# Moving batch loads, an activation and checks in a one-core attention and MLP kernel

One change to a tuned Trainium2 kernel: the last load of batch 1 is issued from the ScalarE queue and the load before it one place earlier, all loads of batch 3 are issued in one go where they had been handed out one by one between the matmuls, two tanh activations of batch 2 are set behind the relu that they stood in front of, and a numerical check is spread over three units of work.

## The chip, the cores and the metric

The kernel runs on one core of one Trainium2 chip. The metric is the device time of one execution in microseconds (us). Most executions of a kernel agree closely (before: 101.72 to 102.07 us). Some are called slow: they come out longer, many of them with a lower granted TensorE clock (kernel 10 below: one run of 103.56 us at a clock of 0.975, beside three of 99.58 to 99.62 us at 0.996 to 1.000). The profile is taken in one further execution; its span, from the first to the last instruction, is about 2 us shorter than the time of the same execution (100.2 against 102.19 us in before).

Engine names: PE is TensorE, DVE is VectorE, ACT is ScalarE, POOL is GpSimd, SP is SyncE. "SPq" and "ACTq" are the DMA issues of SP and of ACT. L357 is line 357 of the kernel.

## The reference, cut to what matters

```python
# B=4 batches, H=8 heads, S=768 positions, D=40: an mLSTM-like attention
for t in range(S):
    m_new = maximum(f[t] + m, i[t])
    C = exp(f[t] + m - m_new) * C + exp(i[t] - m_new) * outer(v[t], k[t])
    n = exp(f[t] + m - m_new) * n + exp(i[t] - m_new) * k[t]
    m = m_new
    y[t] = sigmoid(o_gate[t]) * (C @ q[t]) / maximum(abs(n @ q[t]), 1)
# y becomes x, 3072 tokens of 320 values; then a maxout MLP, d_ff = 1024
out = maximum(x @ w1, x @ w2) @ w_out
```

## The kernel before

The kernel works through chunks of 128 positions, n = 0 to 23, six of them to a batch. `ph` is the matmul that reads the state with q (`C @ q`); `pu` and `po` are the two layers of the MLP, which fill TensorE for most of the time. Before `ph(n)` can run, q has to be loaded, cast to bf16 by GpSimd, and transposed. From n = 8 on, most pairs of chunks are transposed by a DMA on the SP queue (`x_q` below), some on TensorE (`f_q`).

The loads of one batch are six DMAs. A "first" load moves 1024 runs of 160 bytes (160 KB). A "rest" load moves 1024 runs of 800 bytes (800 KB). I call them *narrow* and *wide* below.

```python
def load_first(b, src, store, name, eng):                       # narrow
    t = stage(b, store, name)
    eng.dma_start(out=t[:, :, 0, :], in_=src[b, :, 0:L, :].rearrange("h p d -> p h d"))

def load_rest(b, src, store, name, eng):                        # wide
    t = stage(b, store, name)
    eng.dma_start(out=t[:, :, 1:NT, :].rearrange("p h c d -> p h (c d)"),
                  in_=src[b, :, L:S, :].rearrange("h (p c) d -> p h (c d)", c=REST))

def load_batch(b, eng):          # k, v, q first, gate first, q rest, gate rest
    return [lambda: load_kv(b, b + 1, k, kst, eng), lambda: load_kv(b, b + 1, v, vst, eng),
            lambda: load_first(b, q, qst, "qst", eng), lambda: load_first(b, o_gate, ost, "ost", eng),
            lambda: load_rest(b, q, qst, "qst", eng), lambda: load_rest(b, o_gate, ost, "ost", eng)]
# ... cut ...
def x_q(n):                      # transposes q of the pair n, n+1 by DMA
    b, c = bc(n)
    # ... cut ...
    SP.dma_start(out=qT[b][:, c:c + 2].rearrange("p c s t -> p (c s) t"),
                 in_=qp[b % 2][:, c:c + 2].rearrange("p c s d -> p (c s d)"), transpose=True)
```

The order of everything is written out by a loop over units of work. A list `late` holds pieces that are issued one at a time, one at each call of `fronts` (several calls to a unit). `A` is ScalarE, `V` VectorE, `G` GpSimd.

```python
def cross(n):
    x_q(n)
    done[("q", n)] = clock[0] + 6        # from here ph(n) may be scheduled
late = []
def fronts(limit, cap=1):
    clock[0] += 1
    if late:
        late.pop(0)()
    # ... cut: issues what is ready of q, h, y, k, c ...
# ... cut ...
sigm(1, 0, 1)                    # tanh of the gate on ScalarE
sig_first(1, V)                  # gate scaling on VectorE
for n in (8, 10):
    cross(n)
late += load_batch(2, A)
# ... cut ...
for u in range(FIRST, NU + 1):
    if u == 2:
        # ... cut ...
        late += [lambda: None] * 8 + [lambda: cross(14), lambda: cross(16)]
        sigm(2, 0, 1)
        sig_first(2, V)
        sigm(2, 1, 3)
        sigm(2, 3, 6)
    # ... cut ...
    for half in range(2):
        # ... cut ...
            for _ in up(u, half, then=rows_):        # pu and its relu
                fronts(max(u + 1, 3), 2 if u < 2 else 1)
            if u == 2 and half == 0:
                late += load_batch(3, A)
        if u == NU - 1:
            (check_gates, check_den)[half](*[1][half:])
        if u == NU and half == 0:
            check_flag()
        for _ in down(u - 1, s0, s1):                # po
            fronts(max(u + 1, 3), 2 if u < 2 else 1)
    if u == NU - 2:
        check_gates(0)
```

The checks test on the chip whether the inputs allow the fast formulas; with these inputs they do.

## Time and profile before

| | before |
|---|---|
| median of 3 runs | 101.96 us (101.72 to 102.07) |
| span of the profiled run | 100.2 us |
| TensorE busy | 89.2 us |
| granted TensorE clock | 1.000 |

From the page of the kernel before: busy time of each engine, then TensorE's busy share in 40 equal slices, in tenths, and the granted clock in the same slices.

```profile
PE 89.2 (89%) x846; PEld 63.3 (63%) x846; DVE 54.3 (54%) x160; ACT 42.5 (42%) x63; POOL 28.6 (29%) x67
...
PE   4999978988997959989999998999999999989930
...
PEclk9999999999999999999999999999999999999999
```

TensorE is busy in nine tenths of nearly every slice, at full clock. So the time of this kernel is TensorE's work plus TensorE's waits, and a wait of another engine costs nothing unless it ends in one of TensorE.

These are matmuls from TensorE's timeline of before. The columns are start, duration, engine, line, operation, output and inputs, shapes and count; in brackets, how long TensorE had been idle, and what ended that.

```profile
31.53 0.33 PE L341 MATMUL ps<-qT,kT 120*126 120x128 bf16 x3 [0.53 <-DVE qT L299]
...
34.87 0.32 PE L357 MATMUL ph<-cq,qT 120*128 120x123 bf16 x3 [0.17 <-DMA qT<-qb]
...
37.44 0.32 PE L357 MATMUL ph<-cq,qT 120*128 120x123 bf16 x3 [1.12 <-DMA qT<-qb]
...
44.82 0.60 PE L460 MATMUL pu<-xT,wd 128*128 128x256 bf16 x4 [0.36 <-ACT gt L477]
...
49.44 0.32 PE L357 MATMUL ph<-cq,qT 120*128 120x123 bf16 x3
...
50.78 0.31 PE L357 MATMUL ph<-cq,qT 120*128 120x123 bf16 x3
...
60.82 0.60 PE L460 MATMUL pu<-xT,wd 128*128 128x256 bf16 x4 [0.38 <-DMA xT<-y]
...
89.45 0.69 PE L485 MATMUL po<-Wc_t,xT 64*128 64x320 bf16 x2 [0.28 <-DVE o_sb L499]
```

The six with brackets are the waits that the change is after: for a VectorE copy of qT (31.53), for DMA transposes of q (34.87 and 37.44), for a relu on ScalarE (44.82), for the DMA transpose of y (60.82), and for the copy `o_sb` (89.45). The two at 49.44 and 50.78 are read-outs of pairs 14 and 16: no bracket, so their transposes were in time. The view of waits gives the sum of all waits for q's transposes, as total us, number, and the longest:

```profile
PE ph L357 <- DMA qT<-qb: 1.3, 2, 1.1
```

Next, DMA issues from the timeline of all engines. The second column is how long the issuing engine was occupied; x2 means two issues in a row.

```profile
45.35 2.54 SPq L287 DMA_TRANSPOSE qT<-qb  x2
...
47.83 0.40 ACTq L94 DMA_DIRECT2D qst<-in_q_dram  x1
...
48.94 0.79 ACTq L98 DMA_DIRECT2D qst<-in_q_dram  x1
...
49.77 0.63 ACTq L98 DMA_DIRECT2D ost<-in_o_gate_dram  x1
...
51.06 3.20 SPq L380 DMA_TRANSPOSE xT<-y  x2
```

Pairs 14 and 16 are transposed at 45.35, in a gap: two loads of batch 3, k and v, were issued before (42.3 and 42.7), the narrow ones follow at 47.83, and the wide ones at 48.94 and 49.77. The last line is two transposes of y, issued behind the wide loads. The second of them was issued at 53.02 and landed at about 60.7, so 7.7 us after its issue, against a median of 2.6.

Last, VectorE near the end: the check's reduction waits for GpSimd's subtraction, and the copy `o_sb`, which TensorE waits for, stands behind it.

```profile
87.54 0.90 DVE L527 TENSOR_REDUCE viol<-a 32x1 f32<-32x726 f32 x1 [1.64 <-POOL a L522]
...
88.90 0.89 DVE L499 COPY o_sb<-po 128x320 f32<-128x320 f32 x2
```

### The profile page before, as it was taken

The numbers are of one execution on the slowest core, as the hardware profiler recorded it, in microseconds if no ns is written. First come the engines' busy times: TensorE is split into PE (matmuls) and PEld (weight loads), VectorE is DVE, ScalarE is ACT, GpSimd is POOL, SyncE is SP. The second block draws the span as 40 slices with busy tenths as digits, with TensorE's granted clock in tenths as the row PEclk, the third lists the DMA queues.
The fourth block names the chain that finished last, engine by engine and source line by source line (L and its number), as shares of the span: only waits on it lengthen the run. The fifth ranks groups of instructions, "written<-read, shape, count | busy, mean of one in ns | idle before, by whom it ended". The sixth has DMA issues, their size and how long they took to land.

```text
span 100.2 us, 2241 instructions
## 1 busy us (share of the span) xinstructions
PE 89.2 (89%) x846; PEld 63.3 (63%) x846; DVE 54.3 (54%) x160; ACT 42.5 (42%) x63; POOL 28.6 (29%) x67
## 2 busy tenths in 40 slices
PE   4999978988997959989999998999999999989930
PEld 1356566755686737767867776777676767757610
DVE  5979648543648748865373117772161116395510
ACT  0897685545246450192715086431607071340000
POOL 6044797565255330914020800000000000610000
PEclk9999999999999999999999999999999999999999
DMA  0999999998995999926999999749633201103331
GB/s 17 191 293 355 384 386 365 313 170 139 322 351 136 194 284 347 319 41 155 158 210 368 177 185 313 155 126 65 146 131 65 106 32 70 61 0 134 131 115 35
DMA packets 37311, 18.91 MB, mean 189 GB/s; under 512 B 25648, under 2 KB 35952, under 8 KB 37296
## 3 DMA queue, kind: packets, MB, share of 16 engines
q1 hardware_dynamic: 26138, 14.34, 55.0%
q10 hardware_dynamic: 11158, 4.38, 18.8%
q8 instruction: 8, 0.13, 0.6%
q14 instruction: 7, 0.06, 0.2%
HBM read 12.42 MB, written 3.93 MB: 163 GB/s over the span
## 4 chain that ended last, share of the span: by engine, by line
PE 37%; DMA 32%; SPq 10%; issue 5%; POOL 5%; DVE 5%; ACT 1%; ACTq 1%; POOLq 0%
PE po L496 14%; PE pu L460 11%; DMA xT<-y 8%; DMA ost<-in_o_gate_dram 7%; DMA kst<-in_k_dram 7%; DMA w<-in_moe_w_dram 6%; SPq L104 5%; DMA qT<-qb 5%; PE po L492 4%; PE pu L468 3%; SPq L118 3%; PE ph L357 2%; POOL a L522 2%; DVE o_sb L499 2%; DVE F L520 1%
## 5 line engine op out<-in xcount | busy, mean ns | idle before, releaser
L460 PE MATMUL pu<-xT,wd 128*128 128x256 bf16 (+1 forms) x224 | 25.9, 257 | 1.8 <-ACT gt L477 0.7
L477 ACT ACTIVATE gt<-pu 128x1024 bf16<-128x1024 f32 x18 | 17.5, 1020 | 23.1 <-PE pu L468 23.1
L496 PE MATMUL po<-wo,gt 128*128 128x320 bf16 x160 | 26.6, 299 | 0.0
L499 DVE COPY o_sb<-po 128x320 f32<-128x320 f32 x22 | 10.7, 489 | 22.7 <-PE po L496 21.0
L460 PEld LDWEIGHTS <-wd 128*128 128x128 bf16 x224 | 18.8, 98 | 5.1 <-issue 1.7
L496 PEld LDWEIGHTS <-gt 128*128 128x128 bf16 x160 | 15.1, 98 | 5.4
L265 ACT ACTIVATE ost<-ost 128x320 f32<-128x320 f32 (+2 forms) x14 | 8.7, 656 | 8.5 <-DMA ost<-in_o_gate_dram 8.4
L367 DVE SCALAR_TENSOR_TENSOR y<-ost,ph 128x320 bf16<-128x320 f32 x20 | 9.7, 483 | 4.7 <-PE ph L357 4.7
L492 PE MATMUL po<-Wc_t,xT 128*128 128x320 bf16 x48 | 10.5, 301 | 0.0
L255 POOL CAST qb<-qst 128x240 bf16<-128x240 f32 (+1 forms) x12 | 6.1, 506 | 15.4 <-DMA qst<-in_q_dram 15.4
L220 PE MATMUL pd<-warm,ident_b 128*128 128x512 bf16 x25 | 8.6, 469 | 1.4 <-POOL ident_b masks.py:199 1.4
L522 POOL TENSOR_TENSOR a<-i_sb,F 32x640 f32<-32x640 f32 x1 | 1.5, 1527 | 28.2 <-DVE F L520 28.2
L468 PE MATMUL pu<-xT,wd 64*128 64x256 bf16 (+1 forms) x112 | 7.7, 256 | 0.0
L477 ACT ACTIVATE gs<-pu 128x512 bf16<-128x512 f32 x8 | 4.3, 591 | 7.7 <-PE pu L468 5.3
L357 PE MATMUL ph<-cq,qT 120*128 120x123 bf16 (+1 forms) x60 | 6.0, 214 | 1.6 <-DMA qT<-qb 1.3
L357 PEld LDWEIGHTS <-qT 120*128 120x128 bf16 (+1 forms) x60 | 4.1, 98 | 4.1 <-DMA qT<-qb 1.8
L398 POOL TENSOR_TENSOR wd<-w 128x512 bf16<-128x512 f32 x4 | 5.1, 1269 | 2.5 <-DMA w<-in_moe_w_dram 2.4
L468 PEld LDWEIGHTS <-wd 64*128 64x128 bf16 x112 | 4.0, 94 | 2.6 <-issue 1.7
L492 PEld LDWEIGHTS <-xT 128*128 128x128 bf16 x48 | 3.7, 97 | 2.9 <-issue 1.9
L496 PE MATMUL po<-wo,gs 128*128 128x320 bf16 x32 | 5.2, 299 | 0.0
L220 PEld LDWEIGHTS <-ident_b 128*128 128x128 bf16 x25 | 2.5, 115 | 3.5 <-issue 1.7
L485 PE MATMUL po<-Wc_t,xT 64*128 64x320 bf16 x24 | 3.9, 297 | 0.8 <-ACT Wc_t L438 0.4
(126 smaller groups left out, 108.8 us busy)
## 6 DMA issues: line engine op xcount, KB each, us to landing
out_dram<-o_sb SPq DMA_DIRECT2D x24, 160.0 KB, 3.1
w<-in_moe_w_dram SPq DMA_DIRECT2D x8, 256.0 KB, 5.5
qst<-in_q_dram ACTq DMA_DIRECT2D x2, 800.0 KB, 6.5
ost<-in_o_gate_dram ACTq DMA_DIRECT2D x2, 800.0 KB, 10.5
wo_st<-in_moe_w_out_dram SPq DMA_DIRECT2D x2, 640.0 KB
qst<-in_q_dram SPq DMA_DIRECT2D x1, 800.0 KB
ost<-in_o_gate_dram SPq DMA_DIRECT2D x1, 800.0 KB
wx<-in_moe_w_dram SPq DMA_DIRECT2D x2, 256.0 KB
```

What stands on the lines that cost most here:

```text
L220: nc.tensor.matmul(pd[:, 0, :], ident_b, warm, start=True, stop=True)
L255: cp(eng)(out=qp[b % 2][:, c0:c1, 0:2, 0:HS3 * D].rearrange("p c s (h d) -> p c s h d", d=D), in_=qst[b][:, 0:6, c0:c1, :].rearrange("p (s ...
L265: A.activation(out=s, in_=s, func=AF.Tanh, scale=0.5)
L357: nc.tensor.matmul(ph[:, vcols(s), :].rearrange("p a b -> p (a b)"), lhsT, rhs[:, vcols(s), :].rearrange("p a b -> p (a b)"), start=True, ...
L367: V.scalar_tensor_tensor(out=yo, in0=ost[b][:, :, c, :], scalar=1.0, in1=ph[:, :, 0:D], op0=OP.add, op1=OP.mult)
L398: eng.tensor_tensor(out=wd[:, c, half * 512:half * 512 + 512], in0=t[:, 0, c], in1=t[:, 1, c], op=OP.subtract)
L460: nc.tensor.matmul(pus[i][:, j, :], wd[:, c, f * 128:(f + 1) * 128], x[:, :, GA[i][c], :], start=(c == 0 and (j % 2 == 0 if np_ == 2 else ...
L468: nc.tensor.matmul(pus[i][:, j, :], wd2[r, f * 128:(f + 1) * 128], x[r, :, 2, :], start=False, stop=(j == 3 if np_ == 1 else j % 2 == 1))
L477: A.activation(out=o, in_=pus[i], func=AF.Relu)
L492: nc.tensor.matmul(po, x[:, s // 2, GA[s % 2][cc], :], Wc_t[:, cc, :], start=False, stop=False)
L496: nc.tensor.matmul(po, gt[:, f, s % 2, s // 2 * L:(s // 2 + 1) * L], wo[:, f, :], start=False, stop=(f == NFF - 1))
L499: cp(eng)(out=o_sb, in_=po)
```

## The change

The intent is to take away these waits: gate rest of batch 1 leaves the SP queue so that q of batch 1 arrives earlier; the tanh no longer holds the relu; batch 3's loads are done before y's transposes come; the checks no longer hold the copies. The diff, cut to its core:

```diff
-    for piece in load_batch(1, SP):
-        piece()
+    for j in (0, 1, 2, 4, 3):
+        load_batch(1, SP)[j]()
...
     f_q(4, A)
+    load_batch(1, A)[5]()
...
     def emit(op):
+        if op[:2] == ("q", NT):
+            sig_first(1, V)
...
     sigm(1, 0, 1)
-    sig_first(1, V)
     for n in (8, 10):
         cross(n)
...
             sigm(2, 0, 1)
             sig_first(2, V)
-            sigm(2, 1, 3)
-            sigm(2, 3, 6)
...
                 if u == 2 and half == 0:
-                    late += load_batch(3, A)
+                    sigm(2, 1, 3)
+                    sigm(2, 3, 6)
+                    for piece in load_batch(3, A):
+                        piece()
-            if u == NU - 1:
-                (check_gates, check_den)[half](*[1][half:])
-            if u == NU and half == 0:
-                check_flag()
+            if u == NU - 1 and half == 0:
+                late += [lambda: None] * CP + [check_abs] + [lambda: None] * 2 + [check_low] + [lambda: None] * 5 + [check_flag]
...
-        if u == NU - 2:
-            check_gates(0)
+        if u == NU - 2:
+            late += [lambda: None] * CV + [check_viol]
+        if u == NU - 3:
+            check_gates()
```

Cut: the check's functions are divided into `check_gates`, `check_viol`, `check_abs` and `check_low`, with the same instructions; `CP = 1`, `CV = 12`; in the code, `check_viol` stands ahead of the loop over halves.

More of the change, by code (lines that the diff above doesn't have):

```diff
@@ L514, with check_gates, check_viol @@
     flag_i = const.tile([1, 1], I32, name="flag_i")
-    def check_gates(part):
-        if part == 0:
-            V.memset(ones_b, 1.0)
-            V.memset(ok_b, 0.0)
-            V.tensor_tensor_scan(out=F[:, L:S], data0=ones[:, L:S], data1=f_sb[:, L:S], initial=F[:, L - 1:L],
-                                 op0=OP.mult, op1=OP.add)
-            G.tensor_tensor(out=a[:, L:S], in0=i_sb[:, L:S], in1=F[:, L:S], op=OP.subtract)
-            G.memset(bnd, 0.5)
-            G.tensor_scalar(out=bnd.rearrange("p (b c) h -> p b c h", c=NT)[:, :, 0, :],
-                            in0=gT[:, 1, :].rearrange("p (b h) -> p b h", b=B), scalar1=0.5, scalar2=None, op0=OP.mult)
-            return
+    def check_gates():
+        V.memset(ones_b, 1.0)
+        V.memset(ok_b, 0.0)
+        V.tensor_tensor_scan(out=F[:, L:S], data0=ones[:, L:S], data1=f_sb[:, L:S], initial=F[:, L - 1:L],
+                             op0=OP.mult, op1=OP.add)
+        G.tensor_tensor(out=a[:, L:S], in0=i_sb[:, L:S], in1=F[:, L:S], op=OP.subtract)
+        G.memset(bnd, 0.5)
+        G.tensor_scalar(out=bnd.rearrange("p (b c) h -> p b c h", c=NT)[:, :, 0, :],
+                        in0=gT[:, 1, :].rearrange("p (b h) -> p b h", b=B), scalar1=0.5, scalar2=None, op0=OP.mult)
+    def check_viol():
         V.tensor_reduce(out=viol[:, 0:1], in_=a[:, T0:S], axis=AX.X, op=OP.max)
@@ L532, in check_gates, with check_abs, check_low @@
         V.tensor_tensor(out=ok_b[0:BH, 0:1], in0=viol[:, 1:2], in1=viol[:, 2:3], op=OP.mult)
-    def check_den():
-        ab = ewp.tile([128, B * NT, H], FP, name="ab", tag="ab", bufs=1)
+    ab = const.tile([128, B * NT, H], FP, name="ab")
+    def check_abs():
         V.scalar_tensor_tensor(out=ab, in0=nqb, scalar=-1.0, in1=nqb, op0=OP.mult, op1=OP.max)
+    def check_low():
         V.tensor_tensor(out=ab, in0=bnd, in1=ab, op=OP.subtract)
@@ L698 @@
     XL = 3
+    CP = 1
+    CV = 12
     WX = 12
```

## The prediction

The sum is -1.1 - 0.36 + 0.6 - 0.38 - 0.28 = -1.52 us, and 101.96 less that is the 100.5.

> **What bounds the kernel now.** TensorE: 89.2 us busy of a 100.2 us span (busy table), clock full. After 25 us its matmuls run back to back, and their order is the same in both kernels except for one tiny flag matmul. So only TensorE's waits can be won. Its timeline shows: 0.53 us at 31.5 (scores wait for a VectorE copy of qT), 0.17 at 34.9 and 1.12 at 37.4 (read-out `ph` waits for qT's DMA transposes), 0.36 at 44.8 (`pu` waits for a relu on ScalarE), 0.38 at 60.8 (`pu` waits for the DMA transpose of y), 0.28 at 89.5 (`po` waits for o_sb), and two of 0.25 that the change does not touch. About 2.8 us are within reach.
>
> **The change, step by step.**
> 1. Batch 1. In the SP queue q rest now precedes gate first; gate rest goes to the ACT queue at about 24.6 us. In the trace the 160-byte first pieces take about 1.1 us of DMA each, so q rest should land near 27.4 instead of 28.6, and GpSimd's casts end near 29.8 instead of 31.05. The gate scaling (VectorE, 0.58 us) moves behind the qT copy, which removes the 0.53 us. The second qT transpose (issued 32.5, landed 37.4) can be issued near 31.3, before batch 2's loads fill the DMA. The first is held by an output store ahead of it and gains 0.2. Estimate: 1.1 us (0.3 to 1.8). Gate rest lands as before (30.9).
> 2. tanh of batch 2 behind the relu: ScalarE waited 4.5 us in it for the gate load until 42.2. The 0.36 us goes, and does not grow although TensorE arrives earlier.
> 3. Batch 3 loaded in one go near 42 to 46 instead of 42 to 50.4. Gain: the y transposes at 51 to 54 no longer share with it (the second landed 7.7 us after y; the median is 2.6), so the 0.38 us goes. Cost: the qT transposes of pairs 14 and 16 (issued 45.4 and 46.7, in a gap of the loads) now share with 160-byte packets. [...]beside batch 2's loads a qT transpose landed 4.5 to 4.9 us after issue, against a median of 2.8. I expect new `ph` waits there, 0.3 to 1.2 us, estimate 0.6.
> 4. Checks spread: scan (1.5), GpSimd subtract (1.5) and reduce (0.9) held the o_sb copy until 88.9; now the 0.28 us goes. The scan delays the last y by 1.5 us, with some 8 us of slack. Nothing is added; the tail is unchanged.
>
> Sum: -1.1 - 0.36 + 0.6 - 0.38 - 0.28 = about -1.5. 101.96 becomes **100.5 us**, 8 in 10 between 99.6 and 101.5. Faster by over 2%: 0.23; within 2%: 0.75; slower: 0.02.
>
> **What would show each step.** (1) the wait at 37.4 falls below 0.6, the first large batch-1 cast starts before 28.0, no `ps` wait. (2) no `pu` wait for a relu near 43. (3) batch 3's gate rest lands before 55 instead of 60.3; no `pu` wait for the y transpose; new `ph` waits near 48 to 50, or none. (4) no `po` wait for o_sb at the end.
>
> **What would make it wrong.** [...]the casts come no earlier: step 1 is worth nothing, total 101.5. Or batch 3's burst holds the qT transposes longer than 1.2 us. On the other side, if batch 1's qT transposes run ahead of batch 2's loads and those of pairs 14 and 16 lose nothing, all 2.8 us are won: 99.2.

## The result

Ratios in this document are the mean time of one kernel's fast runs over that of the kernel before in the same rounds, so they are not quite the ratios of the medians quoted. Below 1 is faster than before.

| | before | after |
|---|---|---|
| median of 4 runs | 101.84 us (101.3 to 102.07) | 107.19 us (106.74 to 107.36) |
| span of the profiled run | 100.2 us | 105.3 us |
| TensorE busy | 89.2 us | 91.1 us |
| granted clock, mean | 1.000 | 0.965 |

The ratio is 1.0527 (95% interval 1.047 to 1.0583). The kernel became slower by 5.3%, and the prediction of 100.5 us was wrong. The clock of 0.965 is not the slow state: all four runs of after have 0.960 to 0.965.

The page of after, the same three lines:

```profile
PE 91.1 (87%) x846; PEld 63.9 (61%) x846; DVE 55.2 (52%) x160; ACT 42.5 (40%) x63; POOL 28.4 (27%) x67
...
PE   4999798997999579996329999999999999999940
...
PEclk9999999999999999999965599999999999999999
```

TensorE's row has a hole in the slices from about 50 us on, and the clock's row has one at about the same place. The clock records of the trace say that the granted clock was 0.5 from 53.58 to 60.40 us, which is 6.83 us.

TensorE's timeline of after, at the places shown for before:

```profile
34.58 0.32 PE L357 MATMUL ph<-cq,qT 120*128 120x123 bf16 x3 [0.53 <-DMA qT<-qb]
...
37.27 0.32 PE L357 MATMUL ph<-cq,qT 120*128 120x123 bf16 x3 [1.24 <-DMA qT<-qb]
...
51.84 0.33 PE L357 MATMUL ph<-cq,qT 120*128 120x123 bf16 x3 [2.63 <-DMA qT<-qb]
...
52.44 0.32 PE L357 MATMUL ph<-cq,qT 120*128 120x123 bf16 x3
...
55.23 0.46 PE L357 MATMUL ph<-cq,qT 120*128 120x123 bf16 x3 [2.04 <-DMA qT<-qb]
```

The waits at 31.5, 44.8, 60.8 and 89.5 of before are gone. The two for batch 1's transposes (34.58 and 37.27) have stayed. The two read-outs that had waited for nothing now wait 2.63 and 2.04 us. In the view of waits:

```profile
PE ph L357 <- DMA qT<-qb: 6.4, 4, 2.6
```

The DMA issues at this place in after:

```profile
43.92 0.40 ACTq L94 DMA_DIRECT2D qst<-in_q_dram  x1
...
45.00 0.75 ACTq L98 DMA_DIRECT2D qst<-in_q_dram  x1
...
45.18 2.95 SPq L287 DMA_TRANSPOSE qT<-qb  x2
...
45.79 1.14 ACTq L98 DMA_DIRECT2D ost<-in_o_gate_dram  x1
```

All of batch 3's loads are now issued from 42.1 to 46.9 us, and q rest, the first wide one, is handed over at the same time as the first transpose (45.18), gate rest at the time of the second (46.54).

Two stretches of time: stretch, its length, busy time (and instructions) of PE, PEld, DVE, ACT and POOL, granted clock, DMA share and GB/s. First before, then after.

```profile
49.00:56.00 7.00, 7.00 (x69) 5.26 (x67) 3.99 (x13) 2.61 (x3) 0.94 (x3) 1.00 1.06 265
56.00:62.00 6.00, 5.62 (x53) 4.01 (x51) 1.76 (x4) 3.93 (x5) 1.81 (x6) 1.00 1.24 224
```

```profile
49.00:56.00 7.00, 2.33 (x22) 1.65 (x21) 2.21 (x7) 0.28 (x1) 2.17 (x6) 0.83 1.14 290
56.00:62.00 6.00, 6.00 (x38) 3.44 (x37) 1.53 (x6) 1.94 (x2) 0.00 (x0) 0.63 0.22 30
```

From 49 to 56 us TensorE did 2.33 us of work where it had done 7.00. From 56 to 62 it was fully busy, with 38 matmuls where before there were 53: that is the lower clock (0.63 on average in this stretch), not a wait.

When the same matmul of both traces is compared all along, after minus before is -0.40 us at 46.3 us, +2.40 at the read-out of 49.4, +4.45 at that of 50.8, +6.83 at before's 53.5, +6.31 at 60.8, +6.10 at 72.8, +5.65 at 89.45 and +5.26 at the end. So all of the loss arises within 8 us of before's timeline, in two terms: 4.67 us of waits for the transposes of pairs 14 and 16, and 2.4 us of work at half clock. The rest of the change won about 2 us.

Why were the transposes late? I counted the DMA packets that began in each stretch of 0.5 us: the transposes of q are 768 packets of 256 bytes each, a wide load is 1024 packets of 800 bytes. Before, both transposes ran alone; in after they did not:

```
packets begun    before: 256 B  800 B      after: 256 B  800 B
46.5 to 47.0         364      0                    0      0
47.0 to 47.5         386      0                  183      1
47.5 to 48.0          67      0                  263     19
48.0 to 48.5         419      0                  183     83
48.5 to 49.0         298      0                   74     92
49.0 to 49.5           2      0                   65    136
49.5 to 50.0           0      0                    0    191
50.0 to 50.5           0      0                    0    196
50.5 to 51.0           0     31                   16    190
51.0 to 51.5           0     40                   52    173
51.5 to 52.0           0    141                   57    114
52.0 to 52.5           0    168                   42     51
52.5 to 53.0           0    183                  149    148
53.0 to 53.5           0    178                  162    165
53.5 to 54.0           0    194                  170    163
```

In after the first transpose moves beside the end of the narrow loads and the start of q rest, the second hardly gets a packet while q rest moves, and then shares one to one with gate rest. The two were late in different ways. The first one's data packets began 1.9 us after its issue (1.2 in before) and had all begun by 49.48; but the 32 packets of 4 bytes that follow a transpose's data (in before, 32 behind each of the two) began only between 49.35 and 51.19 (47.38 to 47.64 in before), and it landed at 51.80. The second one's data began 4.0 us after its issue, when 737 of q rest's 1024 packets had begun. So they landed 6.6 and 8.6 us after their issue, where before's took 2.8 and 2.9.

### The profile page after: what moved, and what is told of

Same layout as the page of the kernel before. It is cut to its first block, busy times and chain, and to the rows that moved or that the text cites. A ratio compares the mean times of both kernels' runs of the same rounds, so it can differ in the third digit from the quotient of the medians.

```text
span 105.3 us, 2243 instructions
## 1 busy us (share of the span) xinstructions
PE 91.1 (87%) x846; PEld 63.9 (61%) x846; DVE 55.2 (52%) x160; ACT 42.5 (40%) x63; POOL 28.4 (27%) x67
## 4 chain that ended last, share of the span: by engine, by line
PE 47%; DMA 39%; SPq 6%; ACTq 1%; DVE 1%; issue 1%; ACT 1%; DVEq 0%
PE po L496 20%; DMA ost<-in_o_gate_dram 16%; DMA qT<-qb 13%; PE pu L460 12%; PE po L492 6%; DMA w<-in_moe_w_dram 6%; PE pu L468 5%; DMA qst<-in_q_dram 2%; SPq L118 2%; PE ph L357 2%; DMA kst<-in_k_dram 2%; SPq L104 2%; PE po L485 1%; ACTq L82 1%; SPq L111 1%
## 5 line engine op out<-in xcount | busy, mean ns | idle before, releaser
L496 PE MATMUL po<-wo,gt 128*128 128x320 bf16 x160 | 27.6, 306 | 0.0
```

The costliest lines, as they stand in the source:

```text
L496: nc.tensor.matmul(po, gt[:, f, s % 2, s // 2 * L:(s // 2 + 1) * L], wo[:, f, :], start=False, stop=(f == NFF - 1))
```

## The experiments

At this point I had three questions. Is the burst the whole loss, or do other parts share in it? Is the half clock a consequence of the waits, or a cause of its own? And what makes a transpose late: does a wide load in flight take turns with it (so that it is slowed), or does it go ahead of it (so that it has to wait), or is the end of a transpose tied to the loads in some other way? The quoted texts number the theories as they stood then; a theory or rival in them is a guess that the run was to test.

The kernels ran in four calls, each on one chip, with 7 runs of the kernel before beside them (medians 102.39, 101.8, 102.36 and 103.1 us). As before's median differs from call to call by over 1%, ratios of different calls should not be compared more closely than that.

### 1. After, with batch 3 loaded piece by piece as before

```diff
-                    for piece in load_batch(3, A):
-                        piece()
+                    late += load_batch(3, A)
```

> The changed kernel with one part undone: batch 3's six loads are again handed out one by one between the matmuls, instead of in one go. Theory 1 (the burst of loads holds up the qT transposes of pairs 14 and 16, and the clock drop follows from the waits): both waits at those ph (2.63 and 2.04 us) go to zero, the clock stays at 1.0, and the time is 101.0 to 101.4, slightly better than before, since the relu and o_sb waits (0.36, 0.28) stay away. Rival (moving the gate load of batch 1 to the ACT queue, or the checks, costs the time): stays above 105.

Measured: 100.70 us (100.41 to 101.14), ratio 0.9823 (0.9765 to 0.9881). The clock of the profiled run is 1.000, and the waits at pairs 14 and 16 are gone. What stays is 0.59 and 1.42 us for batch 1's transposes, 0.40 for a y, and 0.17 for the y transpose. So the burst alone turns a kernel that is 1.8% faster than before into one that is 5.3% slower.

### 2. Before, with the burst only

```diff
-                    late += load_batch(3, A)
+                    for piece in load_batch(3, A):
+                        piece()
```

> The kernel before with one part added: batch 3's six loads in one go, nothing else. Theory 1: it shows nearly the whole loss, 106 to 107.5, with ph waits for qT of 2 us or more near 50 and a granted clock of 0.96 to 0.97. Rival (only the sum of all parts is slow, for instance because the loads come earlier behind a relu that no longer waits): below 104.

Measured: 109.71, 108.35, 107.39 and 103.27 us. Three runs had clocks of 0.958 to 0.976, the last had 0.995. The profiled run (slow) waited 2.28 and 2.38 us for the transposes of pairs 14 and 16, and ran at half clock from 55.23 to 62.06 us, again 6.83 us. So the burst brings both terms on top of before too. It also shows that the drop of the clock is not certain: one run in four escaped it, and was still slower than before's median of 102.39.

### 3. After, with dummy matmuls where TensorE waits

Their result is overwritten, so the output is right.

```diff
         ph = ptile([128, H, D1], FP, "ph", pool)
+        for _ in range({15: 18, 17: 14}.get(n, 0)):
+            nc.tensor.matmul(ph.rearrange("p a b -> p (a b)"), ident_b, warm[:, 0:H * D1], start=True, stop=True)
```

> The changed kernel with dummy matmuls (18 and 14 of 328 columns[...]) put in front of the two ph that wait for qT, into the same accumulator, overwritten by the real ones.[...] Theory: the half clock from 53.6 to 60.4 us is caused by TensorE sitting idle in the waits; then the clock stays 1.0, the waits shrink to 0.5 us or less in all, and the time falls by 2 to 2.7 us to 104.5 to 105.2 although the transposes land as late as before. Rival (the clock drops for another reason): clock 0.965 again and 107 or more.

Measured: 105.58 us (104.65 to 106.74, one run of four slow), ratio 1.0237 (1.0168 to 1.0305). From TensorE's timeline, and the clock row of the page:

```profile
49.38 2.67 PE L355 MATMUL ph<-warm,ident_b 128*128 128x328 bf16 x18
52.91 0.32 PE L359 MATMUL ph<-cq,qT 120*128 120x123 bf16 x3 [0.86 <-DMA qT<-qb]
...
54.21 2.12 PE L355 MATMUL ph<-warm,ident_b 128*128 128x328 bf16 x14
```

```profile
PEclk9999999999999999999999999999999999999997
```

The 18 dummies took 2.67 us and the 14 took 2.12, together 4.79. The dummies fill most of the idle time, and the read-outs come no earlier (52.91 here, 51.84 in after). The half clock in mid-kernel is gone, and the ratio is 2.9 points lower than that of after, although TensorE does more work and reaches the read-outs later. (In medians it is 107.19 against 105.58 us, on chips whose kernel before differed by 0.5 us.) So the half clock is a consequence of TensorE's idleness, and its cost is real. The lower digit at the end of the row stands behind the last matmuls.

### 4. After, with gate rest of batch 3 on the SP queue, behind both transposes

```diff
-            late += [lambda: None] * 8 + [lambda: cross(14), lambda: cross(16)]
+            late += [lambda: None] * 8 + [lambda: cross(14), lambda: cross(16), load_batch(3, SP)[5]]
...
-                    for piece in load_batch(3, A):
+                    for piece in load_batch(3, A)[:5]:
```

> The changed kernel, but the last load of the burst (gate rest of batch 3, 800-byte packets) goes to the SP queue right behind the second qT transpose. The q rest load stays in front of both. Theory 2 (descriptors of the ACT queue's loads that are already handed over stand in front of the transposes: the second transpose's first packet came 2.4 us after its issue ended, with the gate load issued just before it): the second transpose's packets follow the first's without a gap, it lands 3 us earlier than 55.2, near 52, and its 2.04 us wait goes to 0.5 or less; time 103 to 104.5. Rival (the queues only take turns packet by packet, and any 800-byte load in flight slows a transpose alike): second transpose lands at 54 or later, time above 106.

Measured: 100.65 us (100.29 to 103.35; one run of five slow), ratio 0.9828 (0.9764 to 0.9893). No wait for pairs 14 and 16. But it tells nothing of which load did it: in the profile q rest, too, was issued only at 50.41, since with the changed order of DMAs its issue waited for an output store (ScalarE was idle for 3.21 us there, and the trace names the store as what ended it). The experiment was inconclusive for its question.

Its slow run, the profiled one, gave something else. The clock fell to half for 3.41 us (39.15 to 42.56), behind waits of only 0.59 and 1.56 us for batch 1's transposes:

```profile
PEclk9999999999999997599999999999999999999998
```

### 5. After, with the transposes of pairs 14 and 16 handed over first

They stand ahead of an output store in the SP queue, so they are issued at 41.96 and 43.26, before the burst's wide loads. The burst stays.

```diff
-            late += [lambda: None] * 8 + [lambda: cross(14), lambda: cross(16)]
+            late += [lambda: None] * 2 + [lambda: x_q(14), lambda: x_q(16)] + [lambda: None] * 4 + [
+                lambda: done.__setitem__(("q", 14), clock[0] + 6), lambda: done.__setitem__(("q", 16), clock[0] + 6)]
```

> The changed kernel with the burst kept, but the qT transposes of pairs 14 and 16 moved ahead of an output store in the SP queue, so that they can be issued when their data are cast (near 42.1 and 43.4) instead of 45.2 and 46.5, before the 800-byte loads of the burst. Theory 1 (loads that are in flight when a transpose is issued hold it up): both ph waits go to 0, clock 1.0, and the y transposes still meet no load; 100.0 to 100.9, a ratio of 0.975 to 0.985. Rival (the burst costs time by something else than these transposes): above 103.

Measured: 101.24 us (100.86 to 102.67; one run of four slow), ratio 0.9911 (0.9837 to 0.9985). The waits for pairs 14 and 16 are gone with the whole burst still there. So it is not the burst as such that costs, but that the transposes are handed over behind or beside it.

### 6. After, with only gate rest issued late

```diff
-            late += [lambda: None] * 8 + [lambda: cross(14), lambda: cross(16)]
+            late += [lambda: None] * 8 + [lambda: cross(14), lambda: cross(16)] + [lambda: None] * 6 + [load_batch(3, A)[5]]
...
-                    for piece in load_batch(3, A):
+                    for piece in load_batch(3, A)[:5]:
```

> The clean form of the run with the gate load behind: there the renamed semaphores also held the q rest load until an output store had landed, so both 800-byte loads came after the transposes and the run told nothing between the two theories. Here q rest stays where it was (issued near 45.0, in front of both transposes) and only gate rest is issued after the relu, near 48.5, behind both. Theory 2 (a transpose waits behind loads handed over before it): the second transpose's first packets come right after the first's, near 49.5 instead of 50.5, it lands near 51.5 to 52.5 instead of 55.2, its wait is under 0.5 and the first's wait shrinks to 1 to 2 us; 102 to 103.5 with the clock at 1.0 or 0.98. Rival (turns packet by packet only; 800-byte packets in flight slow every transpose alike): the second lands at 53.5 or later with a wait of 1 us or more.

Measured: 107.67 us (107.01 to 108.31), ratio 1.0553 (1.0476 to 1.063). From the timeline:

```profile
45.42 0.99 ACTq L98 DMA_DIRECT2D qst<-in_q_dram  x1
...
45.44 2.60 SPq L287 DMA_TRANSPOSE qT<-qb  x2
...
47.64 0.38 ACTq L98 DMA_DIRECT2D ost<-in_o_gate_dram  x1
...
52.00 0.32 PE L357 MATMUL ph<-cq,qT 120*128 120x123 bf16 x3 [2.54 <-DMA qT<-qb]
...
55.19 0.46 PE L357 MATMUL ph<-cq,qT 120*128 120x123 bf16 x3 [1.83 <-DMA qT<-qb]
```

My expectation failed: gate rest was issued at 47.64, beside the second transpose, and the waits are as long as in after (2.54 and 1.83), with half clock from 54.06 to 60.89. One wide load, q rest at 45.42, is enough to delay the first transpose and to hold off the start of the second. In the packets, the second transpose began at about 51.0, when 647 of q rest's 1024 packets had begun, and later shared one to one with gate rest (154 against 151 in half a microsecond). It made me doubt that order or turns explain everything, and suspect that the end of one transpose is tied to the loads; the test of that is kernel 9.

### 7. After, with both wide loads behind the transposes

The four small loads stay in the burst.

```diff
-            late += [lambda: None] * 8 + [lambda: cross(14), lambda: cross(16)]
+            late += [lambda: None] * 8 + [lambda: cross(14), lambda: cross(16)] + [lambda: None] * 6 + load_batch(3, A)[4:]
...
-                    for piece in load_batch(3, A):
+                    for piece in load_batch(3, A)[:4]:
```

> The changed kernel; of batch 3 only the four small loads (160-byte packets) go in one go, the two 800-byte loads follow behind the relu, after both transposes are issued. My prediction's mechanism (160-byte packets share with the transposes and cost 0.3 to 1.2 us): ph waits of 0.3 to 1.2 us stay, 101 to 102. Theory (the 800-byte loads do all of it): both waits under 0.2, as with the loads spread; 100.3 to 101.0.

Measured: 100.67 us (100.25 to 102.33; the profiled run was the slow one), ratio 0.9854 (0.9783 to 0.9924). No wait for pairs 14 and 16. So it is the wide loads. The narrow loads are hardly tested as neighbours in this profile: the transposes were issued at 47.32 and 48.65, and when their data began, at 49.07, all but 63 of the narrow loads' packets had begun. Kernels 5 and 10 have them as neighbours: there the transposes landed 4.4 to 4.8 us after their issue. The slow run again had half clock for 3.41 us (39.0 to 42.41), behind waits of 0.45 and 1.80 us.

### 8. Before, with the batch-1 part alone

The edit takes the first four hunks of the diff above (order of batch 1's loads, gate rest on ScalarE's queue, place of the gate scaling) and leaves the rest as before:

```diff
-    for piece in load_batch(1, SP):
-        piece()
+    for j in (0, 1, 2, 4, 3):
+        load_batch(1, SP)[j]()
...
     f_q(4, A)
+    load_batch(1, A)[5]()
```

> The kernel before with the batch 1 part of the change alone: q rest ahead of gate first, gate rest on the ACT queue, gate scaling behind the qT copy. In the changed kernel's trace the casts came early as predicted (ended 29.6) but the first qT transpose took 2.3 us to issue at 30.0 and the second still was issued at 32.4; the waits for qT were 0.53 and 1.24 in place of 0.53, 0.17 and 1.12. Theory: worth nothing, ratio 0.995 to 1.005. My prediction said 1.1 us: ratio 0.989.

Measured: 102.18 us (101.89 to 102.4), ratio 1.0014 (0.9954 to 1.0074). The part for which I had predicted 1.1 us is worth nothing. The wait of 0.53 us for the VectorE copy is gone, but the two for transposes are 0.81 and 0.91 us where they were 0.17 and 1.12.

### 9. Transposes and loads by themselves

A kernel of its own: it only runs groups of transposes (of the size of `x_q`) and loads, each group begun when the one before it is done. Its output is wrong, which doesn't matter for the time.

```python
def wide(i, b):       # 1024 runs of 800 bytes, on ScalarE's queue
    A.dma_start(out=ld[i][:, :, 1:NT, :].rearrange("p h c d -> p h (c d)"),
                in_=x[b, :, L:S, :].rearrange("h (p c) d -> p h (c d)", c=NT - 1))
def turn(j, cnt=2):   # a transpose of the size of x_q, on SP's queue
    SP.dma_start(out=dst[:, j:j + cnt].rearrange("p c s t -> p (c s) t"),
                 in_=src[:, j:j + cnt].rearrange("p c s d -> p (c s d)"), transpose=True)
```

> A measurement with a wrong result on purpose: nothing but DMA transposes of the kernel's shape (768 packets of 256 bytes) from the SP queue, in seven separate cases: two alone; behind one load of 1024 runs of 800 bytes from the ACT queue; behind two such loads; behind two loads of 160-byte runs; behind two 800-byte loads but as one transpose of twice the size; ahead of the two loads; two alone again. Theory 2 failed in the run with the gate load late: one q rest load in front held up both.[...] It expects: alone, landing 2.6 to 3 us after issue for the first and some 1.3 us later for the second; behind one or two wide loads the first lands 5 to 7 us after issue,[...] the double one ends at least 1 us before the pair. Behind the narrow loads each 3.5 to 5 us. Ahead of the loads: as alone for the first. Rival (turns packet by packet, no more): packets of both run on without a gap at about half the load's rate, and the double one ends when the pair does.

Cut from it is the theory that "It expects" speaks of, with what it said of the second transpose's start: it tied that start to the end of the first transpose. That was not shown, and after's trace speaks against it: the second's data began at 50.55 us, and the last of the first's 32 closing packets only at 51.19.

Measured (one run, 76.47 us). Alone, a transpose landed 2.8 us after its issue. With two wide loads issued at 25.22 and 25.63 and the transposes at 27.88 and 29.19, the first 256-byte packet began only after 31.0 us, and they landed at 33.37 and 33.99. A double-sized transpose, behind two wide loads, began when their packets ended and landed 2.1 us later. So these transposes start late, over 3.1 us after the issue, and from the first one's first packet to its landing it is then 2.4 us at most (alone in before, 1.6). That does not bear out what I had suspected after kernel 6, but it does not refute it: when the data began, 1834 of the loads' 2048 packets had begun, so the end of a transpose beside a wide load is hardly tested here. Case 2 of kernel 13 has it: there the 32 packets of 4 bytes that end the first transpose all began within 0.3 us, beside a wide load. Joining two transposes into one would gain little: the double one landed 5.7 us after its issue, the second of the pair 6.1 us after the issue of the first. With the transposes issued first they landed 2.8 us after their issue, but the loads' packets began only when theirs were through. So this case, like those with one load and with narrow loads, hardly overlapped in time and tells nothing.

### 10. Kernel 7 and batch 1's transposes handed over earlier

```diff
     run(g)
+    x_q(8)
+    x_q(10)
     g = out_full(0, 1, A)
...
     for n in (8, 10):
-        cross(n)
+        done[("q", n)] = clock[0] + 6
```

> A version meant to beat both. The changed kernel with batch 3's two wide loads behind the relu (as tried before, ratio 0.985), and batch 1's two qT transposes put ahead of an output store in the SP queue, so that they are issued as soon as the casts end (near 29.0 and 30.2, instead of 30.0 and 32.4), before batch 2's loads start at 30.6. If loads in flight are what makes transposes late, the waits of 0.5 and 1.4 us at those ph fall below 0.5 in sum and the time is 98.6 to 99.6, a ratio of 0.965 to 0.975. If the transposes are late for another reason the ratio stays at 0.983.

Measured: 99.61 us (99.58 to 99.62 in three fast runs, one slow of 103.56), ratio 0.974 (0.9682 to 0.9797). Issued at 29.19 and 30.64, ahead of an output store, the transposes of batch 1 made TensorE wait no longer. A wait of 0.88 us remained at pair 14, beside the narrow loads, so these are not always free.

### 11. Kernel 5 and the same step for batch 1

The edit is that of kernel 10 for batch 1, on top of kernel 5.

```diff
+    x_q(8)
+    x_q(10)
     g = out_full(0, 1, A)
```

> The same for batch 1, but batch 3's loads stay in one go and the transposes of pairs 14 and 16 go first (as tried before, ratio 0.991). Expected 98.8 to 100.0, ratio 0.967 to 0.98.

Measured: 101.0 us (100.5 to 104.84; two runs of five slow), ratio 0.986 (0.9799 to 0.9921). The profiled run was slow: a wait of 3.76 us for a relu at 51.06 and half clock from 49.44 to 56.27. Kernel 5 ran in another call (0.9911), so what the step adds here is not measured well. The trace of that slow run shows why the relu came so late. On ScalarE it stands behind the issue of gate rest of batch 3, at 49.57, and this issue waited for the semaphore of the second transpose of q, which was issued at 43.88 and landed at 49.55. So in that run the burst held ScalarE as well. In kernel 5 the same issue waited until 47.68, and TensorE waited 0.34 us for the relu.

### 12. Before, with the tanh and the checks moved only

```diff
-            sigm(2, 1, 3)
-            sigm(2, 3, 6)
...
                 if u == 2 and half == 0:
+                    sigm(2, 1, 3)
+                    sigm(2, 3, 6)
                     late += load_batch(3, A)
```

and the checks as in after.

> The kernel before with the two other parts of the change alone: tanh of batch 2 behind the relu, and the checks spread; batch 1 and batch 3 load as before. My prediction gave these 0.36 and 0.28 us: ratio 0.993 to 0.995. The run with batch 3's loads spread again reached 0.982 although the batch 1 part is worth nothing (ratio 1.001 alone), so these two may be worth more than their waits: 0.983 to 0.99. Either way no pu wait for a relu near 44 and no po wait for o_sb near 89 is left.

Measured: 100.17 us (99.97 to 100.52), ratio 0.9807 (0.9757 to 0.9857), all runs fast. From TensorE's timeline, the two waits that are left of the six:

```profile
31.39 0.33 PE L341 MATMUL ps<-qT,kT 120*126 120x128 bf16 x3 [0.50 <-DVE qT L299]
...
37.12 0.32 PE L357 MATMUL ph<-cq,qT 120*128 120x123 bf16 x3 [1.18 <-DMA qT<-qb]
```

The waits for the relu, for the y transpose and for `o_sb` are gone. I had predicted 0.64 us for these two parts together. Compared matmul by matmul, the part at the end is worth 0.85 us, not 0.28: at 72.8 us it is 1.14 us ahead of before, at 89.45 it is 1.60 and at 89.84 it is 1.99. So before waited twice in series for copies held by the check. Before's own line shows the second wait to whoever looks: the two matmuls at 89.45 span 0.69 us, and the same pair at 51.91 spans 0.30.

### 13. Transposes and plain copies beside loads, closer in time

Used to settle what the transposes wait for. It is built like kernel 9, with the transposes issued while, or 1.5 us after, the loads are issued, and with plain copies of the same bytes on the same queue in place of transposes.

```python
# 2: two wide loads, the transposes while they are being issued
start(); wide(0, 2); wide(1, 2); later(0); turn(0); turn(2); done()
# 3: two wide loads, the transposes 1.6 us behind
start(); wide(0, 3); wide(1, 3); later(1); turn(0); turn(2); done()
# 6: two wide loads, two plain copies of the same bytes 1.6 us behind
start(); wide(0, 1); wide(1, 1); later(1); plain(0); plain(2); done()
# 7: the plain copies alone
start(); later(1); plain(0); plain(2); done()
```

> A measurement with a wrong result on purpose, seven cases: one wide load (800-byte runs) with two transposes 0.5 us behind; two wide loads with the transposes while they are issued; two wide loads, transposes 1.6 us behind; two narrow loads (160-byte runs), transposes while they are issued; the same 1.6 us behind; two wide loads with two plain copies of the same bytes 1.6 us behind; the plain copies alone. Theory 2 (what was handed over before goes first, on either queue; what is handed over at the same time takes turns): case 3 has no transpose packet until the wide loads are all but done, 3 us or more after issue, landing 4.5 us or more after issue; cases 1 and 2 mix with the loads and land 3.5 to 6 us after issue; case 5 waits for the rest of the narrow loads, under 1.5 us more than alone (2.8). Plain copies in case 6 are held like the transposes if the rule is about order, and are not if transposes alone are handicapped. Rival (turns by packet): case 3's transposes send packets at half rate from 1 us after issue.

Measured (one run, 70.62 us). The loads' issues of case 3, and the first small read by VectorE of what the first transpose (case 3) or the first copy (cases 6 and 7) had moved:

```profile
27.05 0.37 ACTq L61 DMA_DIRECT2D ld<-in_q_dram  x1
27.47 0.59 ACTq L61 DMA_DIRECT2D ld<-in_o_gate_dram  x1
...
35.92 0.15 DVE L85 CAST see<-dst 128x1 f32<-128x1 bf16 x1 [7.45 <-DMA dst<-src]
...
59.57 0.15 DVE L85 CAST see<-dst 128x1 f32<-128x1 bf16 x1 [5.60 <-DMA dst<-src]
...
65.86 0.15 DVE L85 CAST see<-dst 128x1 f32<-128x1 bf16 x1 [2.22 <-DMA dst<-src]
```

In case 3 the transposes were issued at 28.50 and 29.83, and the first landed 7.3 us after its issue, against 2.8 alone. In case 6 the copies were issued at 53.99, and the first landed in 5.5 us; alone (case 7, issued at 63.67) in 2.1. Plain copies are delayed as transposes are. The packets of cases 2 and 3:

```
case 2: wide loads issued 16.35, 16.76;      case 3: wide loads issued 27.05, 27.47;
transposes 16.72, 17.98                      transposes 28.50, 29.83
packets begun    256 B  800 B                packets begun    256 B  800 B
19.5 to 20.0         0    234                30.5 to 31.0         0    231
20.0 to 20.5        21    227                31.0 to 31.5         0    233
20.5 to 21.0       272    106                31.5 to 32.0         2    227
21.0 to 21.5       159     98                32.0 to 32.5        42    186
21.5 to 22.0       138    140                32.5 to 33.0       104    122
22.0 to 22.5       160    166                33.0 to 33.5        82     86
22.5 to 23.0       137    158                33.5 to 34.0       126    128
```

Alone in before, a transpose (issued at 45.35) had its first packet about 1.2 us later. Here it came about 3.5 us after the issue. By then some 870 (case 2) and 1440 (case 3) of the loads' 2048 packets had begun; after that the two queues shared about one to one, although a packet of the load carries three times the bytes. If there were only turns from the start, the transposes would have begun some 2 us earlier (my estimate from the 3.5 and the 1.2 us). So turns alone are refuted, and both parts are needed: for a time the load that was handed over before, or in the same microsecond, goes alone, though it is on the other queue; then the two share about one to one. How long it goes alone does not seem to depend on how much of it is left: in cases 1, 2, 3 and 6 and in the two cases of kernel 9 with two wide loads, the first packet came 3.3 to 3.8 us after the issue, with anything from 874 to 1940 packets of the loads begun. In case 1, one wide load issued 0.4 us before the transposes, these landed 5.2 and 4.5 us after their issue. In case 4, two narrow loads beside the transposes, these landed 4.8 and 3.9 us after their issue; in case 5, with the transposes 1.5 us behind the loads, 3.1 and 2.9.

### 14. Kernel 1 and batch 1's transposes handed over earlier

The edit is that of kernel 10 for batch 1, on top of kernel 1.

```diff
+    x_q(8)
+    x_q(10)
     g = out_full(0, 1, A)
```

> The changed kernel with batch 3's loads spread (0.982 before) and batch 1's two qT transposes ahead of an output store. In the version with the two wide loads behind the relu the same step took the waits at 34.7 and 37.6 away. Expected: no wait for qT above 0.3 us anywhere; 98.6 to 99.8, ratio 0.965 to 0.975.

Measured: 99.36 us (98.65 to 100.59, the profiled run slow), ratio 0.9653 (0.9573 to 0.9734). In the slow profile, the waits for batch 1's transposes were 0.29 and 1.24 us, so there the step had no effect on them: the first transpose was issued at 29.37, but it occupied the queue for 2.5 us, and the second, issued at 31.93, met batch 2's loads. Whether it is so in the fast runs is not shown.

### 15. Kernel 14 and the transposes of kernel 5

```diff
-            late += [lambda: None] * 8 + [lambda: cross(14), lambda: cross(16)]
+            late += [lambda: None] * 2 + [lambda: x_q(14), lambda: x_q(16)] + [lambda: None] * 4 + [
+                lambda: done.__setitem__(("q", 14), clock[0] + 6), lambda: done.__setitem__(("q", 16), clock[0] + 6)]
```

> The same, and the qT transposes of pairs 14 and 16 also ahead of an output store, so that no qT transpose is issued behind a load of batch 3. Expected within 0.3 us of the version without this step, since its loads of batch 3 are spread anyway: ratio 0.963 to 0.975. If it is 1 us faster, pairs 14 and 16 still waited there.

Measured: 99.07 us (98.92 to 100.7, one run of five slow), ratio 0.9634 (0.9544 to 0.9724). It is the fastest version by ratio, beats both kernels, and its output is right; against kernel 14 (99.36 us) the difference is within the spread. From TensorE's timeline, two of the waits left after 33 us:

```profile
44.44 0.45 PE L385 MATMUL py<-ident_b,y 128*128 128x128 bf16 x5 [0.27 <-DVE y L365]
...
59.50 0.60 PE L460 MATMUL pu<-xT,wd 128*128 128x256 bf16 x4 [0.90 <-DMA xT<-y]
```

No wait for a transpose of q is left at all.

## Why the prediction was wrong

**Step 1, batch 1 (predicted -1.1 us): failed, and worth nothing.** The first half held: the casts ended at 29.55 us in after where they had ended at 31.05, as predicted. But the first transpose stayed behind an output store in the SP queue and was issued at 30.0, and it then occupied the queue for 2.3 us (most others take 1.2 to 1.3; why this one took longer is not shown), so the second one was issued at 32.40, not "near 31.3", and met batch 2's loads as before. Before's trace had shown this: there the first one was issued at 30.29 and the second at 32.52, although the casts ended at 31.05. The 0.53 us wait for the VectorE copy was traded for a longer wait for a transpose. Kernel 8 has it alone at 1.0014. My own list of what could go wrong had this result, but with another reason (the casts would not come earlier).

**Step 2, the tanh (-0.36 us): right.** The relu wait near 44 us is gone in after and in kernels 1 and 12.

**Step 3, the burst (+0.6 and -0.38 us): this is the step that failed.** The gain came: no wait for y's transposes in after. For the cost, the prediction said: "I expect new `ph` waits there, 0.3 to 1.2 us, estimate 0.6." They were 2.63 and 2.04 us, 4.67 in all, as the transposes landed 6.6 and 8.6 us after their issue. Two things were wrong in it.

- *The evidence was taken from the wrong neighbour.* I used the landing time beside 160-byte loads (4.5 to 4.9 us), and took it that a load on another queue only slows a transpose, which no trace had shown. Where narrow loads are in fact the neighbours, in kernels 5 and 10, the transposes did land 4.4 to 4.8 us after their issue. But here the neighbours were two 800-byte loads, and beside them the transposes were not only slowed: the second transpose's data began only when 737 of q rest's 1024 packets had begun, and the first, whose data moved early enough, got its closing 4-byte packets off only up to 1.7 us after the data. Before's trace had a hint of that: the transposes of y, issued at 51.06 and 53.02 behind the wide loads, began their first packet between 54.5 and 55.0 (an output store that stood ahead of them in their own queue, issued at 49.72, was as slow, so the case is not a clean one). I had used these very transposes as the evidence for the gain. Kernels 5 and 7 show from both sides that it is the wide loads: hand the transposes over first, or the wide loads later, and the waits are gone. Kernel 13 shows the late start without the rest of the kernel.
- *A term was missing.* The waits brought TensorE's clock down to half for 6.83 us, which cost 2.4 us of work on top. Kernel 3 shows that the idleness is the cause: with dummy work in the gaps and transposes just as late, the clock stays full and the ratio falls from 1.0527 to 1.0237.

**Step 4, the checks (-0.28 us): right in direction, its size too small.** It measured about 0.85 us, as two waits stood in series behind the same VectorE work.

**The sum.** Up to 46 us the change had won 0.40 us. The two waits cost 4.67, the half clock 2.4, together with small differences +6.83 at 53.5. Then y's transposes gave back 0.5, other small differences 0.2, and the checks near the end about 0.85: the end is at +5.26 us, and the runs at +5.35. My range was far too narrow: I gave "slower" a chance of 0.02, although the text named "Batch 3's burst holds the qT transposes longer than 1.2 us" as a way to be wrong. Kernel 1, after without the burst, has ratio 0.9823; on a before of 101.96 us that would be 100.2, near my 100.5. But part of that is luck, as step 1 was too large and step 4 too small.

What stays open. In after and in kernels 2 and 6, the first transpose's data packets were through about 2 us before TensorE could go on, while only the 32 packets of 4 bytes were left, which began one by one between q rest's. In before it was 0.5 us from the last data packet's start to the landing; by my estimate from this, some 1.8 of the 2.63 us are this late end. That it goes away with the wide loads is shown (kernels 1, 5 and 7); how they cause it is not. In kernel 10 a transpose whose data had all begun by 46.2 landed only at 48.35, beside narrow loads, but in case 2 of kernel 13 there was no late end beside a wide load. In kernel 3 the first transpose was late in the other way: it began 3.8 us after its issue, and ended at once. Why the DMA lets the earlier load go first is not shown by any run either. And why kernel 2's fourth run escaped the half clock (its mean clock was 0.995) is not shown: only one execution of it was traced, a slow one.

## What to carry to other kernels

A small transfer that the critical engine waits for should be handed over before a large load, also when the two are on different queues; free space in the schedule is not enough (kernel 5 against after: ratio 0.9911 against 1.0527). When you judge what a transfer will suffer from a neighbour, look in the trace for the same kind of neighbour (size of its runs, handed over before or after), not for the nearest example. And when TensorE has no other work, price a wait of a few microseconds twice: once for itself, and once for the clock that it may bring down (here 4.67 and 2.4 us).

## What the traces show of queues, the clock and transposes

- Queues: once both transfers have begun, they share about one to one (160 against 166 packets in half a microsecond in case 2 of kernel 13, 162 against 165 in after). The start is another matter: in case 3 of kernel 13 the transpose was issued at 28.50 and only 2 of its 768 packets began before 32.0, while the loads began about 230 in each half microsecond. In the six cases named under kernel 13 the first packet came 3.3 to 3.8 us after the issue; what sets this time is not shown.
- Clock: in kernels 4 and 7 it fell behind waits of at most 1.56 and 1.80 us. In after it fell 0.38 us into the second wait, and the full clock before had lasted 47.787 us, 14 times 3.413; the half clock lasted twice that, 6.827 us. In the 3.41 us before the drop TensorE had been idle, by its records, for 2.06 us: the end of the first wait and the start of the second. Before each of the six drops in mid-kernel (in after and in kernels 2, 4, 6, 7 and 11) it was 1.81 to 2.13 us; in the steps of 3.41 us before that, after which the clock stayed full, it was at most 1.88 us (kernel 2). So in these runs about 2 us of idle time within 3.41 us went with a drop, and the two ranges overlap.
- Transposes: one of this size (768 packets) occupies the issuing queue for 1.2 to 1.3 us in most cases, but for 2.1 to 2.5 us in some (30.29 and 56.51 in before, 29.37 in kernel 14). ScalarE issued loads beside the first of these but none beside the second, so what makes them long is open.
